# The attention step of a fused attention and MoE kernel: other order on TensorE, narrower value matmuls, reordered first loads

## The chip, the cores and the metric

The kernel runs on one core of a Trainium2 chip as one program. The metric is the device time of the whole program in microseconds (us), the median of three runs. Engines are named as in the profile: PE is TensorE, DVE is VectorE, ACT is ScalarE, POOL is GpSimd, SP is SyncE, whose queue (SPq) issues nearly all DMAs here.

## The reference

Two batches, eight heads, 576 positions, head size 64. An attention with a learned position bias is followed by two feed-forward layers of 2048 on 1152 tokens of 512 columns:

```python
scores = (1.0 / np.sqrt(D)) * np.matmul(q, k.transpose(0, 1, 3, 2))
psi_rel = np.log1p(np.abs(rel))                     # rel = pos_i - pos_j
psi_i = np.log1p(np.maximum(pos[:, None], 1.0))
h = np.maximum((psi_rel / psi_i)[..., None] @ w1 + b1, 0.0)   # 32 hidden units for each (i, j)
scores = scores + (h @ w2).transpose(2, 0, 1)[None]            # one bias for each head
attn = np.exp(scores - np.max(scores, axis=-1, keepdims=True))
attn = attn / (np.sum(attn, axis=-1, keepdims=True) + 1e-09)
attn_out = np.matmul(attn, v)
x = moe(attn_out, w_in, w_out)      # h = x @ w_in; relu(h) + alpha * min(h, 0); @ w_out
return moe2(x, w_in2, w_out2)       # h = x @ w_in2; P(h) / (Q(h) + 1e-06); @ w_out2
```

All data are 32-bit floats.

## The kernel before, in words

**Stages.** The attention comes first, then the two feed-forward layers (lines 686 `up` and 701 `down`). Everything is written into one list of pieces, `Agenda`, each with a number that says when it is to come; the pieces are emitted in the order of these numbers, and every engine then works through its own instructions in that order, waiting on semaphores where data or a buffer is not ready. The numbers come from the table `Z` and from `step_time(n)`. They set an order, not a time.

**Steps.** Query rows are cut into nine blocks of 128 (`BLOCKS`: four blocks of rows for each of the two batches, and one last block that holds the 64 left-over rows of both). Each block has four steps, one for each pair of heads, so there are 36 steps, n = 0 to 35. For step n:

- `scores` (line 332, tile `s`): eight matmuls of 288 columns, four for each head.
- `row_max` (line 344, DVE): adds the bias, takes the maximum, leaves the sum in tile `p`.
- `expo` (line 355, ACT): the exponential.
- `flip` (lines 369 and 365, tile `tp`) one step later: nine transposes of 128x128 as 4, 4 and 1, each group into a PSUM tile of the two-buffer pool `ps_t`; `flip_out` copies them into `pt` on ACT (line 381) or DVE (375, 379).
- `values` (line 393, tile `pv`) two steps later: ten matmuls with a stationary tile of 64 columns, which the profile shows as twenty passes; each two of them write the two halves of the 128 output partitions.

A block ends with `inverse`, `inverse_flip` (line 411), `inverse_spread` (lines 418 and 422: a small tile goes to DRAM and comes back spread over the partitions as `rb`), `block_out`, `block_scale` (line 446, DVE) and `block_split`. Blocks from the seventh on use `inverse_on_tensor` (line 438) instead of the way through DRAM.

**Bias.** The bias of a block of rows is made beside the steps of the block before it, one row group (`bias_rows`) for about each step: four `hidden` tiles `h` (line 258 on DVE, line 256 on ACT), then for each half of the 576 columns four matmuls into 32 partitions each (`bias_mm`, line 272, tile `bps`, a PSUM pool of one buffer), then `bias_out` (line 286 on DVE, 284 on ACT; 293 and 291 for the first block) into tile `be`, then a DMA `bias_move` (line 298, or 302) to its place. The first block's eight row groups come before step 0. For the last block `bias_again` (line 306) copies the bias of the first 64 partitions to the other 64.

**Order on PE in a step:** scores, bias half, 4 transposes, values, bias half, 4 + 1 transposes, scores of the next step.

**Widths.** In the rows, `128*128`, `128*64` and `128*32` are rows and columns of the stationary tile of a matmul. Scores and transposes use 128 columns, values 64, bias matmuls 32.

**First loads.** All on SP's queue, in the order of the agenda: small constants, queries of block 0 (`qraw`, a pool of one buffer), four key loads of batch 0 (`kraw`), the rest of the table `tt`, five value loads of batch 0, then the bias moves as their tiles become ready. `be` has three buffers.

Of the kernel before, what the change touches and what calls it, by code (L numbers as in the profile page):

```python
# [22 lines left out]
P = 128  # L23
# [27 lines left out]
def row_tables():  # L51
# [25 lines left out]
    "iflip": 1.64, "ispread": 2.86, "bout": 0.89, "bscale": 1.31, "bsplit": 3.11, "m0": 1.59, "m1": 17.06,  # L77
    "tb": 3.44, "ud": 3.65, "ud2x": 3.05, "ustore": 2.4, "uback": 7.0, "uload": 7.77, "urest": -0.15, "ujoin": 1.2, "utwo_early": 4.81, "ulow_early": 5.57,
# [27 lines left out]
def fused_kernel(ctx: ExitStack, tc: tile.TileContext, qT, q4T, kT, vp, m1_in, m1_out, m2_in, m2_out, small, ttab, out):  # L106
# [46 lines left out]
    xu_p = open_pool("xu", 1, "left")  # L153
    rq_p = open_pool("rq", 1, "left")
    q_p = open_pool("q", 8, "left")
# [3 lines left out]
    h_p = open_pool("h", 10, "right")  # L159
    be_p = open_pool("be", 3, "right")  # L160
    ps_v = open_pool("ps_v", 1, "left", PSUM)
# [79 lines left out]

    bias, hid, bev, bps = {}, {}, {}, {}

# [19 lines left out]
    def bias_mm(j, r, u):  # L263
        if j > 0:
            ps = ps_b.tile([P, HALF], F32, tag="b", name="bps")
            bps[j, r, u] = ps
        else:
            if u == 0:
                bps[j, r] = ps_s.tile([P, 2, 512], F32, tag="s", name="bps2")
            ps = bps[j, r][:, u, :HALF]  # L270
        for c in range(4):
            nc.tensor.matmul(  # L272
                out=ps[32 * c : 32 * c + 32], lhsT=w2s, rhs=hid[j, r, c][:, u * HALF : (u + 1) * HALF],
                start=True, stop=True,
            )
# [28 lines left out]
    def bias_again(h):  # L304

        nc.vector.tensor_copy(out=bias[4][64:, h : h + 4], in_=bias[4][:64, h : h + 4])

    def bias_rows(j, r, at, step, at0, step0):
# [5 lines left out]
        ag.at(at + Z["bias_mm1"] * z, bias_mm, j, r, 1)  # L314
        ag.at(at + (1.6 * step if j == 0 else Z["bias_out1"] * z), bias_out, j, r, 1)
        ag.at(at + Z["bias_move"] * z, bias_move, j, r)

    ptile, pps, tps, ptt, sums, pvs = {}, {}, {}, {}, {}, {}
# [40 lines left out]
    def flip(n, u):  # L359
        p = ptile[n]  # L360
        if u == 0:
            ptt[n] = pt_p.tile([P, 9, P], F32, tag="pt", name="pt")
        tp = ps_t.tile([P, 512], F32, tag="t", name="tp")
        if u == 2:
# [18 lines left out]
    def values(n):  # L383
        k, hp = divmod(n, 4)
        ib, b = BLOCKS[k]
        if hp == 0:
            pvs[k] = ps_v.tile([P, 4, P], F32, tag="pv", name="pv")
        pv, pt = pvs[k], ptt.pop(n)
        for bb, cols in [(b, slice(0, P))] if ib < 4 else [(0, slice(0, 64)), (1, slice(64, P))]:
            for j in range(5):  # L390
                for u in range(2):
                    h = 2 * hp + u
                    nc.tensor.matmul(  # L393
                        out=pv[64 * u : 64 * u + 64, hp, cols],
                        lhsT=V[bb][:, j, h, :],
                        rhs=pt[:, 4 * u + j if j < 4 else 8, cols],
                        start=(j == 0), stop=(j == 4),
                    )
# [91 lines left out]
    for j, r, at, step in rows:  # L490
        bias_rows(j, r, at, step, at0, step0)
        at0, step0 = at, step
    EARLY = rows[-1][2] + Z["bias_move"] * rows[-1][3] / 4.1 + 0.1
    for n in range(NSTEP):
# [11 lines left out]
        if hp == 3:  # L506
            ag.at(t + Z["inv"], inverse, k)
            if by_tensor(k):
                ag.at(t + 3 * DT + Z["bscale"] - 0.1, inverse_on_tensor, k)
            else:  # L510
                ag.at(t + DT + Z["iflip"], inverse_flip, k)
                ag.at(t + DT + Z["ispread"], inverse_spread, k)
            ag.at(t + 3 * DT + Z["bout"], block_out, k)
            ag.at(t + 3 * DT + Z["bscale"], block_scale, k)
            ag.at(t + 3 * DT + Z["bsplit"], block_split, k)
# [280 lines left out]

    ag.at(step_time(20), moe_consts)
    ag.at(EARLY + 2.0, bias_again, 0)
    ag.at(EARLY + 4.0, bias_again, 4)
    ag.at(EARLY, early_pools)  # L800
# [125 lines left out]
```

## Time and profile before

| | before |
|---|---|
| median of 3 runs | 618.4 us (617.63 to 619.54) |
| the profiled execution, its time and its span | 615.66 us, 613.9 us |
| PE busy | 595.5 us, 97% of the span |
| DVE busy | 519.8 us, 85% |
| ACT busy | 436.6 us, 71% |
| share of the chain that ended last | PE 78%, DVE 11%, DMA 5% |
| granted TensorE clock, mean | 0.993 |

Busy time is the time in which at least one instruction of the engine runs. The chain is followed back from the last instruction to what released each piece. Scores start at 26.77 us for step 0 and at 198.25 us for step 35; the first matmul of the feed-forward layers starts at 200.80 us.

### The profile page before, as it was taken

How to read it: one execution, taken by the hardware profiler on the slowest of the kernel's cores; microseconds unless marked ns; L12 is line 12 of the kernel's file. 1: busy time of each engine (PE TensorE's matmuls, PEld its weight loads, DVE VectorE, ACT ScalarE, POOL GpSimd, SP SyncE). 2: the span in 40 equal slices, each digit the busy share in tenths (PEclk: the TensorE clock that was granted, in tenths of full speed). 3: DMA queues.
4: the chain of work that ended last, by engine and by line, in shares of the span. 5: the costliest groups of instructions: out<-in, count | busy, mean ns of one | idle time of the engine just before them, and what ended most of it. 6: DMA issues, size and time to landing. Idle time of an engine off the chain costs nothing.

```text
span 613.9 us, 11091 instructions
## 1 busy us (share of the span) xinstructions
PE 595.5 (97%) x4278; PEld 522.0 (85%) x4278; DVE 519.8 (85%) x883; ACT 436.6 (71%) x724; POOL 77.1 (13%) x83
## 2 busy tenths in 40 slices
PE   8689999999999999999999999999999999999997
PEld 4456667767778999999999999998999999999985
DVE  6799898798688877779998787989999999789783
ACT  4789888889876555777766657787777887655660
POOL 1113222122235332000000020300000000000000
PEclk9889999999999999999999999999999999999999
DMA  9872444323553332445445557775200000001011
GB/s 248 187 198 76 117 118 119 97 72 94 151 152 104 94 113 105 137 130 157 156 146 168 172 167 234 204 253 188 87 1 0 1 2 0 2 0 52 1 52 52
DMA packets 41749, 67.62 MB, mean 110 GB/s; under 512 B 5040, under 2 KB 24800, under 8 KB 41696
## 3 DMA queue, kind: packets, MB, share of 16 engines
q1 hardware_dynamic: 41552, 66.57, 36.9%
q8 instruction: 33, 0.54, 0.4%
q10 hardware_dynamic: 144, 0.35, 0.2%
q14 instruction: 20, 0.16, 0.1%
HBM read 49.71 MB, written 6.58 MB: 92 GB/s over the span
## 4 chain that ended last, share of the span: by engine, by line
PE 78%; DVE 11%; DMA 5%; ACT 2%; issue 2%; POOL 0%; SPq 0%; DVEq 0%; ACTq 0%; POOLq 0%
PE ops L701 29%; PE hps L686 29%; PE bps L272 5%; PE pv L393 5%; PE s L332 4%; PE tp L369 4%; DMA bias<-be 2%; DMA qraw<-in_qT_dram 2%; DVE p L344 1%; DVE mid L625 1%; DVE h L258 1%; DVE w L655 1%; DVE ks L210 1%; DMA away<-mid 1%; DVE acc L773 1%
## 5 line engine op out<-in xcount | busy, mean ns | idle before, releaser
L686 PE MATMUL hps<-xh,w 128*128 128x384 f32 x768 | 204.0, 336 | 0.0
L686 PEld LDWEIGHTS hps<-xh,w 128*128 128x128 f32 x768 | 139.6, 188 | 1.1 <-issue 0.2
L686 PE MATMUL hps<-xl,w 128*128 128x384 f32 x384 | 128.7, 335 | 0.0
L701 PE MATMUL ops<-g,w 128*128 128x384 f32 x576 | 104.5, 336 | 0.0
L701 PE MATMUL ops<-w,g 128*128 128x512 f32 x432 | 102.5, 392 | 1.2 <-DVE acc L773 1.2
L701 PEld LDWEIGHTS ops<-g,w 128*128 128x128 f32 x576 | 100.8, 188 | 0.0
L701 PEld LDWEIGHTS ops<-w,g 128*128 128x128 f32 x432 | 80.7, 188 | 17.5 <-issue 1.5
L686 PEld LDWEIGHTS hps<-xl,w 128*128 128x128 f32 x384 | 72.1, 188 | 0.9
L756 ACT CAST g<-n 128x768 fp32r<-128x768 f32 x48 | 40.1, 835 | 40.0 <-DVE n L720 28.0
L355 ACT ACTIVATE p<-p,nm 128x576 f32<-128x576 f32 x72 | 55.7, 774 | 13.4 <-DVE nm L344 12.9
L272 PE MATMUL bps<-h,w2s 128*32 128x288 f32 x576 | 52.9, 432 | 8.9 <-DVE be L286 3.8
L625 DVE SCALAR_TENSOR_TENSOR mid<-mid,raw 128x512 int32<-128x512 int32 x64 | 48.9, 764 | 13.1 <-ACT mid L617 12.9
L258 DVE TENSOR_SCALAR h<-tt,sc,nb 128x576 f32<-128x576 f32 x98 | 55.8, 605 | 0.1
L344 DVE CUSTOM_DVE_ANT_0 p<-s,bias 128x576 f32<-128x576 f32 x72 | 52.3, 750 | 1.4 <-PE s L332 1.1
L761 DVE TENSOR_TENSOR g<-n,g 128x768 fp32r<-128x768 f32 x48 | 46.6, 970 | 7.8 <-ACT g L756 7.8
L332 PE MATMUL s<-ks,q 128*128 128x288 f32 x320 | 52.4, 308 | 0.6 <-DVE ks L210 0.6
L238 POOL TENSOR_TENSOR q<-qraw,q 128x256 fp32r<-128x256 f32 (+1 forms) x40 | 34.4, 859 | 144.2 <-DVE q L237 124.4
L628 DVE SCALAR_TENSOR_TENSOR mid<-raw,mid 128x512 int32<-128x512 int32 x64 | 49.5, 773 | 2.2
L369 PEld LDWEIGHTS tp<-ident,p 128*128 128x128 f32 x288 | 30.9, 141 | 23.5 <-issue 15.3
L393 PE MATMUL pv<-pt,v 128*64 128x128 f32 (+1 forms) x800 | 47.8, 267 | 0.2 <-DVE pt L375 0.2
L332 PEld LDWEIGHTS s<-ks,q 128*128 128x128 f32 x320 | 44.7, 192 | 2.6 <-issue 1.1
L369 PE MATMUL tp<-ident,p 128*128 128x128 f32 x288 | 46.6, 284 | 0.3 <-ACT pt L381 0.3
(77 smaller groups left out, 836.9 us busy)
## 6 DMA issues: line engine op xcount, KB each, us to landing
raw<-in_moe_w_in_dram SPq DMA_DIRECT2D x32, 512.0 KB, 4.3
raw<-in_moe_w_out_dram SPq DMA_DIRECT2D x32, 512.0 KB, 3.6
bias<-be SPq DMA_DIRECT2D x32, 288.0 KB, 4.8
qraw<-in_qT_dram SPq DMA_DIRECT2D x8, 512.0 KB, 5.5
away<-mid SPq DMA_DIRECT2D x16, 256.0 KB, 2.0
mid<-away SPq DMA_DIRECT2D x16, 256.0 KB, 3.9
v<-in_vp_dram SPq DMA_DIRECT2D x10, 256.0 KB, 7.5
kraw<-in_kT_dram SPq DMA_DIRECT2D x8, 288.0 KB, 5.0
```

What stands on the lines that cost most here:

```text
L258: nc.vector.tensor_scalar(out=h, in0=x, scalar1=sc[:, k : k + 1], scalar2=nb1, op0=ALU.mult, op1=ALU.max)
L272: nc.tensor.matmul(out=ps[32 * c : 32 * c + 32], lhsT=w2s, rhs=hid[j, r, c][:, u * HALF : (u + 1) * HALF], start=True, stop=True,)
L332: nc.tensor.matmul(out=ps[:, w, :HALF], lhsT=x[:, u, :], rhs=kk[:, h, w * HALF : (w + 1) * HALF], start=(i == 0), stop=(i == len(terms) - 1),)
L344: nc.vector.tensor_tensor_reduce(out=ptile[n][:, u, :].rearrange("p (w j) -> p w j", w=2), in0=pps.pop((n, u))[:, :, :HALF], in1=bias[j][: ...
L355: nc.scalar.activation(out=p, in_=p, func=AF.Exp, bias=nms.pop((n, u)), scale=-1.0, accum_out=sums[k][:, h : h + 1])
L369: nc.tensor.transpose(out=tp[:, j * P : (j + 1) * P], in_=p[:, u, o : o + P], identity=ident)
L393: nc.tensor.matmul(out=pv[64 * u : 64 * u + 64, hp, cols], lhsT=V[bb][:, j, h, :], rhs=pt[:, 4 * u + j if j < 4 else 8, cols], start=(j == ...
L625: nc.vector.scalar_tensor_tensor(out=m, in0=m, scalar=3, in1=raw[:, :, 0], op0=ALU.logical_shift_left, op1=ALU.bitwise_or)
L628: nc.vector.scalar_tensor_tensor(out=m, in0=raw[:, :, 1], scalar=-(2 ** 31), in1=m, op0=ALU.bitwise_and, op1=ALU.bitwise_or)
L686: nc.tensor.matmul(out=ps, lhsT=a, rhs=b, start=(i == 0), stop=(i == len(prs) - 1))
L701: nc.tensor.matmul(out=ops[ly, c, m], lhsT=a, rhs=b, start=(f == fs[0] and i == 0), stop=(f == fs[-1] and i == 2))
L761: nc.vector.tensor_tensor(out=gt[:, 1], in0=tmp.pop(p), in1=gt[:, 0].bitcast(F32), op=ALU.subtract)
```

## The change

What it does, part by part:

1. The PE order of a step becomes: scores, all nine transposes of the step before, bias half, values, bias half. The numbers `flip0`, `flip1`, `flip2` put the transposes right behind the scores, and the new `bias_rows_beside` puts the two bias halves on both sides of `values`.
2. `values` uses stationary tiles of 32 columns for all blocks but the last: twenty matmuls in place of ten, each four writing the four quarters of the output partitions.
3. The ninth transpose goes into the upper half of the PSUM buffer of the bias pool `ps_b`, and the first bias half behind it takes the lower half of the same buffer (`spare`).
4. First loads: the third and fourth key load and the five value loads of batch 0 move behind bias moves. `be` gets four buffers, `rq` two, and `load_q` comes earlier in its step.
5. `bias_again` is cut into four copies of two heads, in steps 29 to 32, where it was two copies of four heads.
6. `inverse_flip` moves to just before the scores of step n + 2; `inverse_on_tensor` and its `block_scale` move later in their step.

```diff
-    ... "flip0": 1.82, "flip1": 1.62, ... "flip2": 3.84, "fout2": 4.38, ... "ispread": 2.86,
+    ... "flip0": 0.5, "flip1": 0.1, ... "flip2": 0.7, "fout2": 1.6, ... "ispread": 1.0,
-    ... "load_k02": 3.0, "load_k03": 3.2, ... "load_v0": 4.0, ... "loadq": 5.34,
+    ... "load_k02": 9.5, "load_k03": 11.2, ... "load_v0": 19.3, "again": 2.6, ... "beside": 0.85, "iscale": 2.75, ... "loadq": 2.6,
-    rq_p = open_pool("rq", 1, "left")
+    rq_p = open_pool("rq", 2, "left")
-    be_p = open_pool("be", 3, "right")
+    be_p = open_pool("be", 4, "right")
...
     def bias_mm(j, r, u):
         if j > 0:
-            ps = ps_b.tile([P, HALF], F32, tag="b", name="bps")
+            ps = (spare.pop() if spare else ps_b.tile([P, 512], F32, tag="b", name="bps"))[:, :HALF]
...
-        nc.vector.tensor_copy(out=bias[4][64:, h : h + 4], in_=bias[4][:64, h : h + 4])
+        nc.vector.tensor_copy(out=bias[4][64:, h : h + 2], in_=bias[4][:64, h : h + 2])
...
+    def bias_rows_beside(j, r, at, step, at0, step0):
+
+        z, z0 = step / 4.1, step0 / 4.1
+        for c in range(4):
+            ag.at(at0 + z0 * Z[f"hidden{c}"], hidden, j, r, c)
+        for u in range(2):
+            x = at + Z[f"bias_mm{u}"] * z
+            n = max((n for n in range(NSTEP) if step_time(n) <= x), default=None)
+            t = x if n is None else max(x, step_time(n) + Z["beside"])
+            ag.at(t, bias_mm, j, r, u)
...
+            ag.at(t, bias_out, j, r, u)
+        ag.at(max(at + Z["bias_move"] * z, t + 0.1), bias_move, j, r)
...
-        tp = ps_t.tile([P, 512], F32, tag="t", name="tp")
+        if u < 2:
+            tp = ps_t.tile([P, 512], F32, tag="t", name="tp")
+        else:
+            spare[:] = [ps_b.tile([P, 512], F32, tag="b", name="bps")]
+            tp = spare[0][:, HALF:]
...
+        wide = 32 if ib < 4 else D
...
-                for u in range(2):
-                    h = 2 * hp + u
+                for u, d in [(u, d) for u in range(2) for d in range(0, D, wide)]:
                     nc.tensor.matmul(
-                        out=pv[64 * u : 64 * u + 64, hp, cols],
-                        lhsT=V[bb][:, j, h, :],
+                        out=pv[64 * u + d : 64 * u + d + wide, hp, cols],
+                        lhsT=V[bb][:, j, 2 * hp + u, d : d + wide],
...
-        bias_rows(j, r, at, step, at0, step0)
+        (bias_rows if j == 0 else bias_rows_beside)(j, r, at, step, at0, step0)
...
-                ag.at(t + DT + Z["iflip"], inverse_flip, k)
-                ag.at(t + DT + Z["ispread"], inverse_spread, k)
+                ag.at(step_time(n + 2) - 0.06, inverse_flip, k)
+                ag.at(step_time(n + 2) + Z["ispread"], inverse_spread, k)
...
-    ag.at(EARLY + 2.0, bias_again, 0)
-    ag.at(EARLY + 4.0, bias_again, 4)
+    for h in range(0, H, 2):
+        ag.at(step_time(29 + h // 2) + Z["again"], bias_again, h)
```

On PE, in a step in the middle of the attention, the instructions stood like this before (`s` scores, `bps` bias, `tp` transposes, `pv` values):

```order
L332 MATMUL s<-ks_135,q 128x288 x8
L272 MATMUL bps<-h,w2s 32x288 x4
L369 MATMUL tp<-ident,p 128x128 x4
L393 MATMUL pv<-pt,v_137 64x128 x10
L272 MATMUL bps<-h,w2s 32x288 x4
L369 MATMUL tp<-ident,p 128x128 x4
L365 MATMUL tp<-ident,p 128x128
```

and the same step of the changed kernel stands like this:

```order
L350 MATMUL s<-ks_135,q 128x288 x8
L391 MATMUL tp<-ident,p 128x128 x8
L387 MATMUL bps<-ident,p 128x128
L272 MATMUL bps<-h,w2s 32x288 x4
L415 MATMUL pv<-pt,v_137 32x128 x20
L272 MATMUL bps<-h,w2s 32x288 x4
```

The transposes have moved together behind the scores, values are 20 matmuls of 32 where they were 10 of 64, and bias, values and bias stand next to each other.

On SP's queue the first DMAs were issued in this order before (`sm` constants, `kraw` keys, `tt` the table, `v` values):

```order
L140 DMA sm<-in_small_dram 128x200
L219 DMA qraw<-in_qT_dram 128x1024
L202 DMA kraw<-in_kT_dram 64x1152 x2
L467 DMA tt<-in_ttab_dram 128x472
L202 DMA kraw<-in_kT_dram 64x1152 x2
L213 DMA v_136<-in_vp_dram 128x512 x5
L298 DMA bias<-be 16x8x576 x8
L202 DMA kraw<-in_kT_dram 64x1152 x2
```

and in the changed kernel:

```order
L140 DMA sm<-in_small_dram 128x200
L219 DMA qraw<-in_qT_dram 128x1024
L202 DMA kraw<-in_kT_dram 64x1152 x2
L489 DMA tt<-in_ttab_dram 128x472
L298 DMA bias<-be 16x8x576 x2
L202 DMA kraw<-in_kT_dram 64x1152
L298 DMA bias<-be 16x8x576
L202 DMA kraw<-in_kT_dram 64x1152
L298 DMA bias<-be 16x8x576 x5
L213 DMA v_136<-in_vp_dram 128x512 x5
```

The first bias moves now stand ahead of the value loads and of two key loads.

On DVE near the end of the attention, the rows between the maxima of steps 28 and 29 (`p,nm` is `row_max`) were these before:

```order
L344 ISA p,nm<-s,bias 128x576
L344 ISA nm 128x1
L306 COPY bias<-bias 64x2304
L237 CAST q<-qraw 128x256
L306 COPY bias<-bias 64x2304
L375 COPY pt<-tp 128x128
L344 ISA p,nm<-s,bias 128x576
```

and in the changed kernel the first such copy stands one step later, behind the maxima of step 29, alone:

```order
L362 ISA p,nm<-s,bias 128x576
L362 ISA nm 128x1
L397 COPY pt<-bps 128x128
L237 CAST q<-qraw 128x256
L306 COPY bias<-bias 64x1152
L401 COPY pt<-tp 128x512
L362 ISA p,nm<-s,bias 128x576
```

One copy of 1152 elements stands there now, and three more of that size follow in later steps.

## Rows read from the trace of the kernel before

**Rows 1.** Windows: start:end, length, busy us (instructions) of PE, PEld, DVE, ACT, POOL, PEclk, DMA.

```profile
32.36:75.35 42.99, 40.76 (x419) 27.37 (x415) 39.72 (x94) 37.87 (x75) 11.57 (x9) 0.97 0.52 139
75.35:165.93 90.58, 90.58 (x998) 64.52 (x997) 75.56 (x204) 77.81 (x164) 20.52 (x24) 1.00 0.39 104
270.00:400.00 130.00, 130.00 (x749) 130.00 (x748) 114.18 (x174) 88.78 (x148) 11.49 (x8) 1.00 0.58 174
```

**Rows 2.** The same windows, PE, scores alone (line 332, eight a step).

```profile
32.36:75.35 42.99, 11.69 (x65) 0.97 0.52 139
75.35:165.93 90.58, 24.74 (x152) 1.00 0.39 104
```

**Rows 3.** The same window, PE, bias matmuls alone (line 272, eight passes a half).

```profile
75.35:165.93 90.58, 24.93 (x288) 1.00 0.39 104
```

**Rows 4.** Timeline of PE, one step (start, length, line, tile, shape, passes).

```profile
111.71 1.31 PE L393 MATMUL pv<-pt,v 128*64 128x128 f32 x20
112.95 0.69 PE L272 MATMUL bps<-h,w2s 128*32 128x288 f32 x8
113.57 0.66 PE L369 MATMUL tp<-ident,p 128*128 128x128 f32 x4
...
114.09 1.29 PE L332 MATMUL s<-ks,q 128*128 128x288 f32 x8
115.32 0.69 PE L272 MATMUL bps<-h,w2s 128*32 128x288 f32 x8
115.94 0.66 PE L369 MATMUL tp<-ident,p 128*128 128x128 f32 x4
116.53 0.66 PE L393 MATMUL pv<-pt,v 128*64 128x128 f32 x8
```

**Rows 5.** Timeline of PE, a late step that has no bias matmuls.

```profile
179.19 1.30 PE L332 MATMUL s<-ks,q 128*128 128x288 f32 x8
180.32 0.60 PE L369 MATMUL tp<-ident,p 128*128 128x128 f32 x4
180.85 1.31 PE L393 MATMUL pv<-pt,v 128*64 128x128 f32 x20
...
182.62 2.37 PE L332 MATMUL s<-ks,q 128*128 128x288 f32 x16
```

**Rows 6.** Timeline of PE, two bias halves side by side before step 0.

```profile
23.18 1.18 PE L272 MATMUL bps<-h,w2s 128*32 128x288 f32 x16
```

**Rows 7.** Timeline of PE, values of the last block (half as many columns each).

```profile
196.41 1.39 PE L393 MATMUL pv<-pt,v 128*64 128x64 f32 x40
```

**Rows 8.** The start: timeline of DVE, of SP, the chain, landing of bias moves.

```profile
19.27 0.82 DVE L293 TENSOR_SCALAR be<-bps,cv 128x576 f32<-128x576 f32 x1 [3.81 <-DMA bias<-be]
...
4.68 4.85 SPq L213 DMA_DIRECT2D v<-in_vp_dram  x5
...
10.50 7.21 DMA bias<-be
...
DMA to landing us min/median/max: 3.3/4.8/6.0
```

**Rows 9.** Waits from 75.35 to 165.93: who for whom, us in total, times, longest.

```profile
ACT be L284 <- PE bps L272: 11.6, 16, 1.2
```

**Rows 10.** Waits from 26 to 76.

```profile
DVE q L237 <- DMA qraw<-in_qT_dram: 0.9, 1, 0.9
```

**Rows 11.** Timeline of PE and DVE, steps 29 and 30.

```profile
169.03 1.35 DVE L306 COPY bias<-bias 64x2304 f32<-64x2304 f32 x1 [0.62 <-DMA bias<-be]
169.46 1.30 PE L332 MATMUL s<-ks,q 128*128 128x288 f32 x8
174.58 1.30 PE L332 MATMUL s<-ks,q 128*128 128x288 f32 x8
```

**Rows 12.** Timeline of DVE and SP, the way of the inverse through DRAM.

```profile
111.39 0.27 DVE L413 COPY rt<-tp 8x128 f32<-8x128 f32 x1
112.92 1.27 SPq L422 DMA_DIRECT2D rb<-rd  x2
```

More of the change, by code (lines that the diff above doesn't have):

```diff
@@ L74 @@
     "bias_out0": 1.51, "bias_mm1": 3.37, "bias_out1": 3.67, "bias_move": 6.78, "dt2": 4.01, "row2": 3.98,
[2 rows of a table removed]
-    "iflip": 1.64, "ispread": 2.86, "bout": 0.89, "bscale": 1.31, "bsplit": 3.11, "m0": 1.59, "m1": 17.06,
[2 rows of a table added]
+    "iflip": 1.64, "ispread": 1.0, "bout": 0.89, "bscale": 1.31, "bsplit": 3.11, "m0": 1.59, "m1": 17.06,
     "tb": 3.44, "ud": 3.65, "ud2x": 3.05, "ustore": 2.4, "uback": 7.0, "uload": 7.77, "urest": -0.15, "ujoin": 1.2, "utwo_early": 4.81, "ulow_early": 5.57,
@@ L240, in split_q @@
             )
-    bias, hid, bev, bps = {}, {}, {}, {}
+    bias, hid, bev, bps, spare = {}, {}, {}, {}, []
     def bias_tile(j):
@@ L314, in bias_rows @@
         ag.at(at + Z["bias_mm1"] * z, bias_mm, j, r, 1)
-        ag.at(at + (1.6 * step if j == 0 else Z["bias_out1"] * z), bias_out, j, r, 1)
+        ag.at(at + 1.6 * step, bias_out, j, r, 1)
         ag.at(at + Z["bias_move"] * z, bias_move, j, r)
+    def bias_rows_beside(j, r, at, step, at0, step0):
[7 more added lines that the diff above has]
+            ag.at(t, bias_mm, j, r, u)
+            if n is None:
+                t += 0.4
+            else:
+                key = "scalar" if f"bias_scalar_{j}{u}" in ON else "vector"
+                t = max(step_time(n) + Z[f"bo_{key}{int(t - step_time(n) >= Z['values'])}"], t + 0.1)
+            ag.at(t, bias_out, j, r, u)
+        ag.at(max(at + Z["bias_move"] * z, t + 0.1), bias_move, j, r)
     ptile, pps, tps, ptt, sums, pvs = {}, {}, {}, {}, {}, {}
@@ L362, in flip @@
             ptt[n] = pt_p.tile([P, 9, P], F32, tag="pt", name="pt")
-        tp = ps_t.tile([P, 512], F32, tag="t", name="tp")
+        if u < 2:
+            tp = ps_t.tile([P, 512], F32, tag="t", name="tp")
+        else:
+            spare[:] = [ps_b.tile([P, 512], F32, tag="b", name="bps")]
+            tp = spare[0][:, HALF:]
         if u == 2:
@@ L508, in fused_kernel @@
             if by_tensor(k):
-                ag.at(t + 3 * DT + Z["bscale"] - 0.1, inverse_on_tensor, k)
+                ag.at(t + 3 * DT + Z["iscale"] - 0.1, inverse_on_tensor, k)
             else:
-                ag.at(t + DT + Z["iflip"], inverse_flip, k)
-                ag.at(t + DT + Z["ispread"], inverse_spread, k)
+                ag.at(step_time(n + 2) - 0.06, inverse_flip, k)
+                ag.at(step_time(n + 2) + Z["ispread"], inverse_spread, k)
             ag.at(t + 3 * DT + Z["bout"], block_out, k)
-            ag.at(t + 3 * DT + Z["bscale"], block_scale, k)
+            ag.at(t + 3 * DT + Z["iscale" if by_tensor(k) else "bscale"], block_scale, k)
             ag.at(t + 3 * DT + Z["bsplit"], block_split, k)
```

10 rows, old and new, of the table Z are left out of this document.

## The prediction

> **What bounds the kernel now.** I read the busy times first: PE is busy 97% of the span, and the chain that ended last is PE for 78%. So I looked at the windows, to see where in the attention PE is the limit and where it isn't. From 270 to 400 us, in the feed-forward layers, PE is busy in every microsecond [rows 1]: nothing in the change touches them, and whatever the attention gains or loses, they start that much earlier or later. The attention has four stretches.
>
> From 75.35 to 165.93 us PE is also busy without a gap, 90.58 of 90.58 us, while DVE is busy for 75.56 and ACT for 77.81 [rows 1]. The scores count 152 matmuls, eight a step [rows 2]: 19 steps of 4.77 us, of which DVE needs 3.98 and ACT 4.10. ACT waits 11.6 us in all for bias matmuls [rows 9]. Here PE's order and widths set the time. From 32.36 to 75.35 the 65 score matmuls are eight steps of 5.37 us [rows 1, 2]; DVE is busy for 39.72 of 42.99 us, so DVE sets that time, with PE close behind it (40.76). Before step 0, DVE sits idle for 3.81 us because `be` isn't free: the bias move that frees it was issued at 10.50 and took 7.21 us, behind five value loads that were issued from 4.68 on [rows 8]. And at the end, steps 29 to 31 are uneven (below).
>
> **The order on PE, steps 75 to 166.** One step before, from start to start [rows 4]: values 1.24 (111.71 to 112.95), bias 0.62, five transposes 0.52, scores 1.23 (114.09 to 115.32), bias 0.62, four transposes 0.59 (115.94 to 116.53); 4.82 in all.
>
> Some of that belongs to changing the width of the stationary tile. Scores followed by transposes (128 columns, then 128) take 1.13, from 179.19 to 180.32 [rows 5]; followed by bias (128, then 32) they take 1.23 [rows 4]: 0.10 for leaving a width. Four transposes behind scores take 0.53, from 180.32 to 180.85 [rows 5]; behind bias they take 0.59 [rows 4]: 0.06 for entering one. Two bias halves side by side last 1.18 [rows 6] where one lasts 0.69 [rows 4], so the second adds 0.49, and not 0.62: the same size again. I take 0.16 a change. A step had five changes of width (scores to bias, bias to transposes, transposes to values, values to bias, bias to transposes) and has two after: transposes to bias, and bias to scores.
>
> The new step, piece by piece: scores 1.13 + 0.06 for entering = 1.19; nine transposes, with 0.107 each from (0.53 - 0.10) / 4, plus 0.10 for leaving = 1.07; first bias half 0.62 - 0.10 = 0.52; values 1.24 - 0.16 = 1.08; second bias half 0.62 - 0.06 = 0.56. Sum 4.42, so 0.40 less a step. Three changes at 0.16 would give 0.48, the upper end.
>
> The 1.08 holds only if four value parts of 32 columns run side by side as two of 64 do. No row shows that form. Below: twenty passes of 128 columns, one after the other at the 0.107 of a transpose, would take 2.1, and took 1.24 [rows 4], so two do run side by side; and a bias half, eight passes of 288 columns, adds 0.49 [rows 6] where one after the other would take 8 x 0.107 x 288 / 128 = 1.9, so four parts of 32 do. Above: forty passes, as many as there will be, last 1.39 in the last block [rows 7], against 1.31 for twenty [rows 4]: 0.08 more. Between 1.08 and 1.16 I take 1.08, since the bias row is the same tile form; with 1.16 the step saves 0.32.
>
> A page speaks against this part. The Trainium skill, "TensorE: Matmul & The Clock Gate", section "Wait — 56ns, not 53.3ns?", says that with hardware decode off the sequencer spends about 62 ns on each matmul and becomes the limit once the array's work is shorter. By that figure forty passes would take 40 x 62 = 2.48 us, an estimate from that page. The trace disagrees: its forty passes last 1.39 us [rows 7], 35 ns each.
>
> Then ACT (4.10) and DVE (3.98) are only 0.3 and 0.4 below the new 4.42. Steps differ (a block's end adds work on both), so some wait will remain; I take off 0.08 a step. All 19 steps have a pair of bias halves but one (288 passes are 36 halves [rows 3]). **19 x 0.32 = 6.0 us**; bounds 19 x 0.16 = 3.0 (values at 1.16 and a doubled hold) and 18 x 0.48 = 8.6.
>
> What is queued behind the moved pieces: the transposes wait for the second exponential of the step before, and bias and values now stand behind them. That exponential follows a maximum which can start when the scores are done, and has until the next step's scores end, over 5 us later, so I cost it at nothing; in a step of 5 us it is covered too. The second bias half needs the shared buffer read by `flip_out` and the first `bias_out`; values, 1.08, lie between.
>
> **The first 32 us.** The value loads go behind the bias moves, and `be` has four buffers, so the move of row group 0 has to land only before the fifth row group is written out. The move issued at 10.50 then takes 3.3 to 6.0 as others do [rows 8] and lands at 13.8 to 16.5; DVE stopped at 19.27 - 3.81 = 15.46. So between 2.8 and 3.8 of the 3.81 goes, and DVE has no other wait of such a size before step 0. I take 3.8, the nearer to the usual landing of 4.8, plus 0.3 for PE which no longer stands still there: **4.1 us**, bounds 2.8 and 4.8. Two key loads fall behind two bias moves, some 9 us later, and are cast only after 25 us; the value loads have some 15 us until the first `values`: nothing.
>
> **Steps 0 to 8.** DVE's work is unchanged, at 39.72 of 42.99 us [rows 1]: at most 3.3 can go. One wait that surely goes is the 0.9 for queries [rows 10], by the second `rq` buffer. I take **1.2 us**, bounds 0 and 2.8.
>
> **The end.** Steps 29 to 30 take 5.12 (169.46 to 174.58) [rows 11]; a step without bias takes 3.43, from 179.19 to 182.62 [rows 5]. The two copies of `bias_again`, 1.35 each, start at 169.03 after a 0.62 wait for a bias move [rows 11], and the maximum of step 29 stands behind both. In the change it stands behind none, the wait is a step later, when the move has landed, and each later step carries one copy of half the size, about 0.7, below what DVE has free. 5.12 - 3.43 = **1.7 us**; bounds 0.4 (the copies delay later maxima instead) and 2.8.
>
> **Sum.** 6.0 + 4.1 + 1.2 + 1.7 = 13.0 us. The profiled execution took 615.66, which would become 602.7; the median of the runs shown is 618.4, 2.7 above it, so I forecast **605.4 us**. All lower bounds add to 6.2 (612.2), all upper ones to 19.0 (599.4).
>
> **Rivals.**
> - *Values become slow.* If the four parts run as two pairs, one pair after the other, values cost 1.08 more. In 19 steps that is 20.5; in the eight before, PE has 2.2 to spare of 42.99 [rows 1], so 6.4 of 8.6 count: 27 in all, against 13: 632 us, slower. It decides from about 0.5 us a step on. Against it: the bias rows. The page's 62 ns would make it 1.4 a step, near 640 by the same count, an estimate from that page.
> - *The changes of width don't go away*, as bias and values, though both 32 wide, differ in what they read and where they write: the step stays at 4.8, and 7.0 us remain: 611.4.
> - *ACT or DVE take over.* Their 77.81 and 75.56 leave room, but if the order makes them wait as often as now (11.6 us over 19 steps, 0.6 a step [rows 9]), steps come to 4.10 + 0.6 = 4.7, and about 5 of the 6.0 is lost: 610.
> - *The inverse comes late.* From its copy at 111.39 to the end of the second `rb` issue at 114.19 it takes 2.8 [rows 12], and landing 3.3 or more [rows 8]. It now starts just before the scores of step n + 2, and `block_scale` on DVE, with a maximum queued behind it, comes about 1.4 steps later, 6.2 us: up to 1 us late in six blocks, and later behind a query load. 13 - 6 = 7: 611.
> - *More than I count:* 0.48 a step with no hold, and DVE's idle time of steps 0 to 8 all gone: 8.6 + 4.8 + 2.8 + 2.0 = 18: 600.
>
> **How the numbers follow.** Forecast, 602 to 609: 0.62. More: 0.10. Width changes stay: 0.07. ACT or DVE: 0.09. Inverse: 0.07. Slow values: 0.05. The range is 599.5 to 611.5: it takes in the sum's upper bound and the rivals that leave 7 us, and leaves out slow values and mishaps together. 0.3% of 618.4 is 1.9 us, which is what a measurement of this kernel can tell from no change. Faster 0.92, same 0.03 (two of the middle rivals together), slower 0.05.
>
> **What would show it.** Values behind bias should start about 0.5 after it, and last near 1.1 from start to start, with forty passes; a step should take 4.4 to 4.5 between 70 and 155 us, and ACT's wait for bias matmuls shrink. DVE's 3.81 idle should be gone and the first scores start near 23. No copy of bias should stand ahead of the maximum of step 29. The forecast is wrong if values last 1.3 or more, if DVE waits for `rb`, or if transposes wait long for exponentials.

## The result, and the profile after

| | after |
|---|---|
| median of 4 runs | 627.5 us (625.4 to 629.33) |
| before, same chip, 4 runs | 618.97 us (617.63 to 619.71) |
| ratio | 1.0139, 95% interval 1.0097 to 1.0182: slower |
| profiled execution, its time and span | 629.33 us, 627.5 us |
| PE busy | 596.7 us, 95% |
| chain that ended last | PE 68%, DVE 13%, issue 6%, DMA 5%, ACT 5% |
| granted TensorE clock, mean | 0.984 |

The forecast was 605.4. The two profiled executions stand further apart than the medians, by 13.67 us against 8.5: the one after is the slowest of its four (628.73 and 629.33 us at mean clocks of 0.982 and 0.984, 625.4 and 626.26 at 0.991 and 0.992), and the one before lies 3.3 us under its median. To see where the 13.67 us arose, I noted when the scores of a step start, and took the stretches between them:

| stretch | before | after | difference | forecast |
|---|---|---|---|---|
| up to the scores of step 0 | 26.77 | 24.50 | -2.27 | -4.1 |
| step 0 to step 8 | 43.71 | 55.92 | **+12.21** | -1.2 |
| step 8 to step 28 | 95.45 | 98.20 | **+2.75** | -6.0 |
| step 28 to step 35 | 32.32 | 32.23 | -0.09 | -1.7 |
| step 35 to the end | 415.63 | 416.70 | +1.07 | 0 |

First the windows of the changed kernel, from step 1 to 8, from 8 to 28 and from 28 to 35 (start:end, length, then busy us and instructions of PE, PEld, DVE, ACT, POOL, then PEclk, DMA share and GB/s):

```profile
30.97:80.42 49.45, 39.64 (x484) 28.61 (x480) 36.71 (x81) 32.88 (x66) 10.26 (x8) 0.83 0.51 130
80.42:178.62 98.20, 92.01 (x1454) 70.04 (x1450) 78.23 (x217) 82.84 (x174) 22.44 (x26) 1.00 0.34 95
178.62:210.85 32.23, 30.63 (x460) 26.82 (x456) 27.05 (x69) 22.87 (x51) 13.13 (x22) 1.00 0.51 141
```

PE was never idle from 75 to 166 us [rows 1]; now, from step 8 to 28, it is idle for 6.2 us of 98.2. In the seven steps from 1 to 8 it stands for 9.8 of 49.45 us, where in the eight from 1 to 9 it stood for 2.23 of 42.99 [rows 1]. DVE and ACT have idle time as well there: no engine is the limit. They wait for one another.

**A step that nothing disturbs**, PE's timeline (start, length, line, tile, shape, passes), to be held against [rows 4]:

```profile
120.08 1.35 PE L350 MATMUL s<-ks,q 128*128 128x288 f32 x8
121.27 1.04 PE L391 MATMUL tp<-ident,p 128*128 128x128 f32 x8
122.14 0.27 PE L387 MATMUL bps<-ident,p 128*128 128x128 f32 x1
122.34 0.69 PE L272 MATMUL bps<-h,w2s 128*32 128x288 f32 x8
122.85 1.27 PE L415 MATMUL pv<-pt,v 128*32 128x128 f32 x40
123.99 0.69 PE L272 MATMUL bps<-h,w2s 128*32 128x288 f32 x8
...
124.64 0.64 PE L350 MATMUL s<-ks,q 128*128 128x288 f32 x3
```

From start to start: scores 1.19, nine transposes 1.07, bias 0.51, values 1.14, bias 0.62, a small inverse transpose 0.03; 4.56 us in all. I had 1.19, 1.07, 0.52, 1.08 and 0.56, 4.42. So PE's own work came out almost as costed. Twenty such steps would be 91.2 us; they took 98.2.

**A step from 80 to 179 us that is long** (109.22 to 115.18, 5.96 us): DVE, ACT and PE in turn. In brackets stand the idle time before and who ended it.

```profile
111.91 0.69 DVE L468 TENSOR_TENSOR xu<-xu,rb 128x512 f32<-128x512 f32 x1 [0.87 <-DMA rb<-rd]
112.52 0.75 DVE L362 CUSTOM_DVE_ANT_0 p<-s,bias 128x576 f32<-128x576 f32 x1
...
113.68 0.28 DVE L397 COPY pt<-bps 128x128 f32<-128x128 f32 x1
```

```profile
114.00 0.50 ACT L284 ACTIVATE be<-bps,cv 128x288 f32<-128x288 f32 x1 [1.59 <-DVE pt L397]
```

```profile
111.97 1.27 PE L415 MATMUL pv<-pt,v 128*32 128x128 f32 x40
114.56 0.69 PE L272 MATMUL bps<-h,w2s 128*32 128x288 f32 x8 [1.32 <-ACT be L284]
115.18 1.05 PE L350 MATMUL s<-ks,q 128*128 128x288 f32 x6
```

This reads as a chain. DVE stands 0.87 us for `rb`; its scaling (`block_scale`), a maximum and a hidden tile come ahead of the copy of the ninth transpose; ACT's `bias_out`, in the same buffer as that transpose, waits for the copy; the second bias half needs the buffer and waits for ACT; and the next scores stand behind that bias half on PE. So one late DMA reaches the scores.

**The early steps.** PE, DVE and ACT from step 1 on:

```profile
34.37 0.41 PE L387 MATMUL bps<-ident,p 128*128 128x128 f32 x1
34.71 0.73 PE L272 MATMUL bps<-h,w2s 128*32 128x288 f32 x8
39.06 1.19 PE L272 MATMUL bps<-h,w2s 128*32 128x288 f32 x8 [3.62 <-DVE be L286]
40.18 1.33 PE L350 MATMUL s<-ks,q 128*128 128x288 f32 x4
41.31 1.93 PE L391 MATMUL tp<-ident,p 128*128 128x128 f32 x8
```

```profile
35.52 0.29 DVE L397 COPY pt<-bps 128x128 f32<-128x128 f32 x1 [1.59 <-PE bps L272]
35.85 1.35 DVE L210 TENSOR_TENSOR ks<-kraw,ks 64x1152 fp32r<-64x1152 f32 x1
37.23 0.76 DVE L362 CUSTOM_DVE_ANT_0 p<-s,bias 128x576 f32<-128x576 f32 x1
...
37.91 0.58 DVE L258 TENSOR_SCALAR h<-tt,sc,nb 128x576 f32<-128x576 f32 x1
38.40 0.51 DVE L286 TENSOR_SCALAR be<-bps,cv 128x288 f32<-128x288 f32 x1
```

```profile
40.33 0.50 ACT L284 ACTIVATE be<-bps,cv 128x288 f32<-128x288 f32 x1 [5.02 <-PE bps L272]
```

The first bias half ends at 35.4. DVE copies the ninth transpose out only then, although that transpose had been made by 34.78: both are in one buffer. Of the 1.59 us that DVE is idle before the copy, 0.7 come after the transpose's end. Then a key cast, a maximum and a hidden tile run on DVE, and `bias_out` comes at 38.40. PE's second bias half waits 3.62 us for it, with the scores of step 2 behind it; ACT waits 5.02 us for that half. The Trainium skill has a rule that fits the copy's wait: "PSUM — Partial Sum Buffer", section "PSUM bank collisions raise a hardware error", tells to guard PSUM by bank and quadrant and not by address, so two halves of one bank don't make two independent buffers. The waits agree: 5.0 us in 8 such waits of DVE's copy in the row of the waits below.

The waits of steps 1 to 8 and of steps 8 to 28 (who for whom: us in total, times, longest):

```profile
ACT be L284 <- PE bps L272: 11.4, 3, 5.0
PE bps L272 <- DVE be L286: 5.6, 2, 3.6
PE bps L272 <- ACT be L284: 3.5, 3, 1.7
```

```profile
ACT be L284 <- DVE pt L397: 6.0, 10, 1.6
PE bps L272 <- ACT be L284: 5.6, 7, 1.4
DVE pt L397 <- PE bps L272: 5.0, 8, 1.1
DVE xu L468 <- DMA rb<-rd: 2.2, 2, 1.3
```

In steps 1 to 8 PE waits 9.1 us in all for `bias_out`, on DVE or ACT, nearly its whole idle time of 9.8. Before, its waits for `bias_out` on DVE from 26 to 76 us, step 0 included, were these, with 0.3 more for ACT:

```profile
PE bps L272 <- DVE be L286: 3.8, 5, 2.1
```

PE's 5.6 us for ACT between 80 and 179 are nearly its whole idle time there (6.2).

**The start.** DVE:

```profile
22.14 0.82 DVE L293 TENSOR_SCALAR be<-bps,cv 128x576 f32<-128x576 f32 x1 [1.75 <-DMA bias<-be]
```

The wait of 3.81 [rows 8] became 1.75, for another move. In the chain it stands like this:

```profile
14.42 7.62 DMA bias<-be
```

It took 7.62 us, hardly other than the 7.21 in [rows 8], though no value load was ahead of it any more; two key loads and three bias moves were, issued from 10.44 us on. From 14 to 22 us the DMA engines were full (start:end, as in the windows above; the share of DMA is the last column but one):

```profile
14.00:22.00 8.00, 7.94 (x87) 3.85 (x86) 6.26 (x13) 7.67 (x10) 0.73 (x1) 1.00 1.04 207
```

**The end.** From step 29 to 30 it took 3.47 us (182.11 to 185.58), where it had taken 5.12 [rows 11]: the 1.65 that I had costed at 1.7. From 31 to 32 it took 4.55 (before 3.43), and from 34 to 35 7.07 (before 5.74), which gave it back.

### The profile page after: what moved, and what is told of

Its sections match the earlier page's. It is cut to its first block, busy times and chain, and to the rows that moved or that the text cites. A ratio compares the mean times of both kernels' runs of the same rounds, so it can differ in the third digit from the quotient of the medians.

```text
span 627.5 us, 12390 instructions
## 1 busy us (share of the span) xinstructions
PE 596.7 (95%) x4918; PEld 529.4 (84%) x4918; DVE 518.9 (83%) x885; ACT 436.6 (70%) x724; POOL 78.0 (12%) x83
## 4 chain that ended last, share of the span: by engine, by line
PE 68%; DVE 13%; issue 6%; DMA 5%; ACT 5%; POOL 1%; SPq 0%; DVEq 0%; ACTq 0%; POOLq 0%
PE ops L723 28%; PE hps L708 28%; PE bps L272 4%; PE s L350 3%; PE tp L391 3%; DVE p L362 2%; PE pv L415 2%; DVE h L258 2%; DMA rb<-rd 1%; DMA bias<-be 1%; DVE mid L647 1%; DVE ks L210 1%; DMA qraw<-in_qT_dram 1%; ACT h L256 1%; ACT p L373 1%
## 5 line engine op out<-in xcount | busy, mean ns | idle before, releaser
L350 PE MATMUL s<-ks,q 128*128 128x288 f32 x320 | 57.3, 323 | 2.6 <-DVE ks L210 2.6
L350 PEld LDWEIGHTS s<-ks,q 128*128 128x128 f32 x320 | 46.9, 200 | 15.3 <-issue 15.1
L415 PEld LDWEIGHTS pv<-pt,v 128*32 128x32 f32 (+1 forms) x1440 | 40.6, 113 | 8.0 <-issue 2.6
L415 PE MATMUL pv<-pt,v 128*32 128x128 f32 (+1 forms) x1440 | 46.5, 268 | 0.0
L643 ACT ACTIVATE raw<-raw 128x512 int32<-128x512 uint32 x64 | 43.4, 678 | 3.7 <-DMA raw<-in_moe_w_out_dram 2.8
```

Source lines behind the costliest of these rows:

```text
L350: nc.tensor.matmul(out=ps[:, w, :HALF], lhsT=x[:, u, :], rhs=kk[:, h, w * HALF : (w + 1) * HALF], start=(i == 0), stop=(i == len(terms) - 1),)
L415: nc.tensor.matmul(out=pv[64 * u + d : 64 * u + d + wide, hp, cols], lhsT=V[bb][:, j, 2 * hp + u, d : d + wide], rhs=pt[:, 4 * u + j if j ...
L643: nc.scalar.activation(out=low, in_=low.bitcast(U32), func=AF.Copy, scale=0.90625 * 2.0 ** -29, bias=0.24)
```

## The experiments

All times are medians of 4 to 10 runs; beside them the median of before on the same chip. The three stretches are of the profiled execution, in us. Before had 26.77, 43.71 and 95.45, the changed kernel 24.50, 55.92 and 98.20.

| kernel | time | before | ratio (95%) | to step 0 | 0 to 8 | 8 to 28 |
|---|---|---|---|---|---|---|
| e1_old_order | 618.9 | 617.3 | 1.0025 (0.9998 to 1.0052) | 25.00 | 44.28 | 99.23 |
| e2_values64 | 625.47 | 617.3 | 1.011 (1.0047 to 1.0173) | 23.74 | 52.95 | 98.40 |
| e3_old_loads | 627.27 | 617.3 | 1.0141 (1.0065 to 1.0218) | 25.36 | 52.20 | 97.65 |
| e5_whole_scores | 628.93 | 617.3 | 1.0165 (1.0099 to 1.023) | 25.07 | 52.63 | 98.61 |
| e4_old_inverse | 628.84 | 616.72 | 1.0196 (1.0142 to 1.0251) | 24.64 | 53.88 | 99.03 |
| e6_old_order_inverse | **610.93** | 616.72 | 0.9899 (0.9847 to 0.9952) | 23.71 | 43.47 | 92.91 |
| e7_loads_only | 613.5 | 616.72 | 0.9948 (0.9926 to 0.997) | 24.87 | 44.44 | 95.47 |
| e8_new_order_late | 618.1 | 616.72 | 1.0021 (0.9997 to 1.0045) | 24.10 | 44.18 | 98.65 |
| e9_later_scale | 621.18 | 617.04 | 1.0066 (1.0037 to 1.0095) | 24.33 | 55.63 | 93.71 |
| e10_mixed_later_scale | 614.26 | 617.04 | 0.9949 (0.993 to 0.9968) | 24.49 | 44.02 | 94.88 |
| e11_ninth_apart | 626.37 | 617.04 | 1.013 (1.0089 to 1.0171) | 24.12 | 48.62 | 101.55 |
| e12_bias_on_act | 623.17 | 617.04 | 1.0082 (1.0059 to 1.0105) | 23.80 | 47.68 | 100.09 |
| e13_both_links | 617.61 | 617.55 | 0.9993 (0.9969 to 1.0017) | 25.27 | 47.23 | 94.68 |

Six kernels keep the new order in all steps and its shared buffer and its writers of bias (the changed one, e2, e3, e4, e5 and e9): their steps 0 to 8 take 52.2 to 55.9, so the early loss against 43.71 is 8.5 to 12.2 us, by execution. By medians, two pairs of kernels that were run together give it: e4 and e8 differ in the order of steps 0 to 7 alone (the ninth transpose's buffer goes with it), by 10.7 us, and e9 and e10 in that and in the time of one block's inverse, by 6.9.

**e1_old_order: PE's order, bias places and the ninth transpose as before**, in the changed kernel; values of 32, loads, pools and the new time of the inverse stay.

```diff
-    ... "flip0": 0.5, "flip1": 0.1, ... "flip2": 0.7, "fout2": 1.6, ...
+    ... "flip0": 1.82, "flip1": 1.62, ... "flip2": 3.84, "fout2": 4.38, ...
...
-        (bias_rows if j == 0 else bias_rows_beside)(j, r, at, step, at0, step0)
+        bias_rows(j, r, at, step, at0, step0)
```

> The changed kernel with the order of before on all engines for transposes and bias, and the ninth transpose back in its own tile; values of 32 columns, first loads, pools, bias copies and inverse stay as changed. Theory of the ring (in the new order the second bias half waits for ACT's and DVE's readers of the one bias tile, with the next scores queued behind it, and the scores of steps 1 to 3 are cut in two by the transposes): the 12 us lost between steps 0 and 8 and the 0.14 a step lost behind them go, step 8 starts about 44 us after step 0, and the time is 612 to 618. Theory of the loads (the value loads, now at 23 to 28 us, keep the DMA engines full until 44 us and what waits for them late): the loss stays before step 4, time 624 to 629. Theory of slow values (32 columns): the steps from 8 on stay at 4.9 or more, time over 622.

618.9, just above the range of the ring: the early loss is gone (44.28), but steps 8 to 28 are no faster (99.23). Ordinary steps take 4.67 us, and one in each block 5.8 to 7.1, in which the inverse's transpose, now just ahead of the scores, waits for a buffer of `ps_t` (waits of steps 8 to 28):

```profile
PE tp L429 <- ACT pt L399: 5.5, 5, 1.3
DVE xu L464 <- DMA rb<-rd: 1.4, 1, 1.4
```

**e2_values64: values as before** (`wide = D`), all else as changed.

> The changed kernel with values of 64 columns again, all else as changed. Ring: the step is held by waits and by 4.50 of PE work; with 64 columns PE's work rises by two changes of width, to about 4.8, part of which the waits swallow: 2 to 6 us slower than the change, 629 to 634. Slow values: faster than the change by 3 us or more. Loads: as the ring has it.

625.47, not above the changed kernel: a miss. Against before it is 1.011, where the changed kernel is 1.0139, and the two intervals overlap. In the new order the narrow values gain nothing over steps 8 to 28 (98.40 with 64 columns, 98.20 with 32), though undisturbed steps take 4.70 to 4.76 with 64 and 4.56 with 32. That the waits between the engines swallow this fits, but no run tests it by itself.

**e3_old_loads: the first loads in the order of before.**

```diff
-    ... "load_k02": 9.5, "load_k03": 11.2, ... "load_v0": 19.3, ...
+    ... "load_k02": 3.0, "load_k03": 3.2, ... "load_v0": 4.0, ...
```

> The changed kernel with the two key loads and the value loads of batch 0 issued first again, as before; four buffers of be and two of rq stay. Loads: the 12 us lost between steps 0 and 8 go, the first scores start near 26, time 616 to 619. Ring: the loss between steps 0 and 4 stays at 9 us or more, the first scores start 1 to 2 us later than the change's 24.5, time 627 to 631.

627.27, with 52.20 from step 0 to 8: the moved loads don't make the early loss. The start is 0.9 later.

**e5_whole_scores: transposes behind the scores of both heads also in steps 1 to 3 and 33 to 35**, where the changed kernel puts them between the heads (the timeline above: scores x4, transposes x8).

> The changed kernel with the transposes emitted behind both heads' scores in steps 1 to 3 and 33 to 35 too (their time counted from the next step's own start), all else as changed. If the ring of the early steps closes through the cut scores (maximum of the second head waits for scores that stand behind eight transposes): steps 1 to 4 become 1 to 2 us shorter each, 4 to 7 us in all, time 620 to 624. If the ring closes through the bias tile alone: 1 to 2 us, time 625 to 627. Loads: no change.

628.93, above both expectations. Steps 0 to 8 take 52.63, within the 52.2 to 53.9 of e2, e3 and e4, which keep the cut: the cut isn't the cause.

**e4_old_inverse: the inverse at the time of before**, in the new order.

```diff
-    ... "ispread": 1.0, ...
+    ... "ispread": 2.86, ...
...
-                ag.at(step_time(n + 2) - 0.06, inverse_flip, k)
-                ag.at(step_time(n + 2) + Z["ispread"], inverse_spread, k)
+                ag.at(t + DT + Z["iflip"], inverse_flip, k)
+                ag.at(t + DT + Z["ispread"], inverse_spread, k)
```

> The changed kernel with inverse_flip and inverse_spread at their times of before, all else as changed. If the late inverse (DVE waits for rb with a maximum and the copy of the ninth transpose behind it) makes the long steps of 5.9 to 6.1 us: three or four of them shrink to about 4.6, time 621 to 624. If the bias tile alone holds the steps: under 2 us, time 625 to 628.

628.84, a miss: the wait for `rb` is gone, but the inverse's transpose now comes right behind eight others and waits for ACT to copy one of their tiles out (waits of steps 8 to 28):

```profile
PE tp L433 <- ACT pt L403: 4.7, 5, 1.4
```

**e6_old_order_inverse: e1 and e4 together**, so that of the change there remain values of 32, loads, pools, bias copies and the later `inverse_on_tensor` of the last blocks.

> Order of before for transposes, bias and inverse; of the change only values of 32 columns, first loads, pools and bias copies. In the run with the old order and the late inverse, ordinary steps took 4.67 us where before has 4.83, and one step of each block 5.8 to 6.2, PE waiting at the inverse's transpose for ACT to free a transpose tile. If that wait is all that held it back: no long steps, 19 steps of 4.67 between 75 and 166 us, time 609 to 613. If the long steps have another cause: 617 to 620.

610.93, faster than both kernels. PE is busy again without a gap from step 8 to 28 (windows, steps 0 to 8 and 8 to 28):

```profile
23.71:67.18 43.47, 39.56 (x509) 26.48 (x509) 41.12 (x91) 36.28 (x69) 12.24 (x9) 0.92 0.80 191
67.18:160.09 92.91, 92.84 (x1453) 68.21 (x1451) 80.04 (x217) 82.61 (x175) 21.54 (x25) 1.00 0.37 100
```

**e7_loads_only: e6 with values of 64.**

> As the kernel with order and inverse of before, and with values of 64 columns too: only first loads, pools and bias copies of the change are left. If 32 columns save one change of width a step (values to bias): 3 to 5 us slower than that kernel, 613 to 617, steps of 4.83. If the narrow values save nothing: the same as that kernel. Against before this gives the worth of loads, pools and bias copies: my prediction's terms for the start and the end say 5 us less, the first runs say about 2.

613.5. The narrow values are worth 2.6 us, and what else e6 keeps of the change 3.2. Steps 8 to 28 take 95.47 against 92.91: 0.13 a step on the mean, and 0.15 in ordinary steps (4.82 against 4.67), for one change of width less.

**e8_new_order_late: e6, with the new order from step 8 on** (order of before in steps 0 to 7).

```diff
+    EARLY_STEPS = 8
...
-        (bias_rows if j == 0 else bias_rows_beside)(j, r, at, step, at0, step0)
+        (bias_rows if at < step_time(EARLY_STEPS) else bias_rows_beside)(j, r, at, step, at0, step0)
...
+            f0, f1, f2, o2 = (1.82, 1.62, 3.84, 4.38) if n < EARLY_STEPS else (0.5, 0.1, 0.7, 1.6)
...
```

> The new order from step 8 on and the order of before in steps 0 to 7, inverse at its time of before; the rest as changed. If the new order costs only where PE has to wait for a DVE that is full (steps 0 to 8): the early 10 us come back and steps from 8 on take 4.5 to 4.6, time 606 to 611, the fastest of all. If the ring through the bias tile costs the same in a PE-bound step as it saves: steps of 4.7 to 4.8, 611 to 617.

618.1, above both expectations: steps 0 to 8 are as in e6 (44.18), steps 8 to 28 as in e4 (98.65), 5.74 more than in e6. The order costs in both places, in the later one with the inverse's transpose behind eight others, as in e4.

**e9_later_scale: the changed kernel with `block_scale` and `block_split` of the first six blocks later in their step.**

```diff
-    ... "bscale": 1.31, ...
+    ... "bscale": 3.0, ...
...
-            ag.at(t + 3 * DT + Z["bsplit"], block_split, k)
+            ag.at(t + 3 * DT + (Z["bsplit"] if by_tensor(k) else 4.9), block_split, k)
```

> The changed kernel, with block_scale and block_split of the first six blocks placed about 1.7 us later in their step, so that DVE does not stand at rb when the scaling comes. If the late inverse (a wait of 1.3 us for rb on DVE, and what queues behind it) makes the long steps of 5.9 to 6.1 between steps 8 and 28, they shrink and steps 8 to 28 take 93 to 95.5 us instead of 98.2: 621 to 625. If the ring over the shared bias buffer (copy of the ninth transpose behind the bias half, bias_out behind that copy, second bias half behind bias_out) makes them, the waits only change their name: 626 to 629.

621.18. Steps 8 to 28 fall from 98.20 to 93.71; the step from 109 to 115 takes 4.56 (108.34 to 112.90). DVE no longer waits for `rb`, and PE's waits for ACT go from 5.6 to 2.6:

```profile
PE bps L272 <- ACT be L284: 2.6, 5, 1.4
```

So DVE's wait for the late inverse, 2.2 us, is worth 4.5 us here, passed on.

**e10_mixed_later_scale: e8, with the new inverse and the later scaling from step 8 on.**

> The order and inverse of before in steps 0 to 7, the new order and new inverse from step 8 with the later scaling; everything else as changed. The early loss of 11 to 12 us must be gone in any case (scores of step 8 near 68). If late rb is all that keeps the new order from its 4.5 a step, steps 8 to 28 take 90 to 93 us: 606 to 611. If the order of the pieces itself costs waits in the steps, they take 95 to 99: 612 to 618.

614.26, in the range of the second theory; 94.88 from step 8 to 28, just under what it had there, and still 2 more than e6. PE still waits 2.7 us there for ACT's `bias_out`, and none in e6.

**e11_ninth_apart: the ninth transpose in its own buffer**, and back behind the second bias half, in the changed kernel. So it changes the buffer and the place at once.

```diff
-    ... "flip2": 0.7, "fout2": 1.6, ...
+    ... "flip2": 3.84, "fout2": 4.38, ...
...
-        if u < 2:
-            tp = ps_t.tile([P, 512], F32, tag="t", name="tp")
-        else:
-            spare[:] = [ps_b.tile([P, 512], F32, tag="b", name="bps")]
-            tp = spare[0][:, HALF:]
+        tp = ps_t.tile([P, 512], F32, tag="t", name="tp")
```

> The changed kernel, with the ninth transpose back in a PSUM tile of its own pool, behind the second bias half as before; the bias pool's one buffer is then used by bias halves alone. If sharing one buffer between the ninth transpose and the first bias half closes the ring (the copy waits for the bias half, bias_out for the copy), both the early loss and the steps from 8 to 28 shrink: 612 to 620. If the order itself does it (bias halves ahead of and behind the values, the second one waiting for bias_out, with the next scores queued behind), it stays at 625 to 629.

626.37: half a hit. Steps 0 to 8 take 48.62, so 4 to 7 us of the early loss come from the ninth transpose in the bias buffer, its place included; but steps 8 to 28 grow to 101.55, as the inverse's transpose now waits for `ps_t`. In the early steps PE still waits for DVE's `bias_out`:

```profile
PE bps L272 <- DVE be L286: 4.6, 3, 2.5
```

**e12_bias_on_act: the bias of the second row block, which is made beside steps 0 to 7, written out on ACT alone** (`"bias_scalar_11"` added), in the changed kernel. The halves that move from DVE to ACT are the second halves of the 576 columns; in the changed kernel's trace they stand first in steps 0 to 2, and second from step 3 on.

> The changed kernel, with the first bias halves' bias_out of the second row block (steps 0 to 7) written out on ACT too, where half of them were on DVE. If the early ring closes because DVE's bias_out stands behind the casts, maxima and hidden tiles that DVE has in these steps, the early loss of 12 us shrinks by 3 to 8 us: 619 to 624. If any engine's bias_out is too late for the second bias half, it stays near 627, or ACT's queue makes it longer, up to 632.

623.17, as the first theory had it: steps 0 to 8 take 47.68, 4.5 to 8 less, though steps 8 to 28 take 100.09. DVE's `bias_out` behind its cast and maxima is the other link.

**e13_both_links: e11 in steps 0 to 7, e12 and e9 together.**

> The changed kernel with the two links of the early ring broken together (in steps 0 to 7 the ninth transpose in its own tile behind the second bias half, and bias_out of the second row block's first halves on ACT too), and the later block_scale for the steps behind. If these two links and the late rb are the whole loss, steps 0 to 8 take 44 to 45.5 us as in the order of before and steps 8 to 28 take 93 to 95.5: 610 to 615. If putting both bias halves beside values is itself too tight in the early steps, whoever writes them out, steps 0 to 8 keep 47 to 49 us: 616 to 620.

617.61, no faster than before, as the second theory had it. Steps 0 to 8 still take 47.23, 3 to 4 more than in the order of before; the medians say the same, 3.4 us above e10, which has the order of before in these steps and the same later scaling. What is left has the same name, with ACT in DVE's place (waits of steps 0 to 8):

```profile
PE bps L272 <- ACT be L284: 7.5, 7, 4.6
```

## Why the prediction was wrong

**The step that failed** is "What is queued behind the moved pieces". It costed the transposes' wait for exponentials at nothing, and gave no cost at all to what it says last, that "the second bias half needs the shared buffer read by `flip_out` and the first `bias_out`; values, 1.08, lie between". That wait came to 9.1 us on PE from step 1 to 8 and 5.6 from 8 to 28. 1.08 us isn't enough for DVE's copy and a `bias_out` that stand in their engines' order behind maxima, casts and hidden tiles, and in steps 0 and 1 there are no values at all. Before, four transposes and the values lay between the two halves, 1.8 us, and five transposes and the scores between the second half and the next first one, also 1.8 [rows 4]. Now it is 1.14 between the halves and 2.26 behind the second, and the scores are queued behind that half. Putting the old order back in steps 0 to 7 removes the early loss (e8, e10); breaking either link of the ring removes a part (e11, e12), and both together don't remove all (e13). So the order itself is the cause, sharpened by the shared buffer and by DVE's queue.

**The inverse that comes late** was a rival at 0.07, priced at up to 1 us in six blocks. It came, for 4.5 us in steps 8 to 28 (e9), beside the failed step and not in its place; of the prediction's signs of being wrong, it is the one that showed: DVE waits for `rb`. In the order of before the new time costs about 8 us (e1 against e6), there also through a transpose that finds no free buffer.

**The new order on PE** was rightly costed as work: 4.56 a step for 4.42. Mis-sized were values (1.14 for 1.08) and the second bias half (0.62 for 0.56). A change of width cost 0.15 in ordinary steps where it was isolated (e6 against e7; I took 0.16), and the further two that the new order saves only 0.05 each (4.67 to 4.56). The four parts of 32 do run side by side. So the rival of slow values and that of widths that don't go away both fall.

**The hold of 0.08 a step** was too small: the steps from 8 to 28 lose (98.20 - 91.2) / 20 = 0.35 each. I argued from busy times that ACT and DVE had 0.3 and 0.4 to spare; that a step's chain passes through PE, DVE, ACT and PE again in one step doesn't show in busy times. The rival in which ACT or DVE take over, at 0.09, had such waits too, but with these engines as the limit; in steps 8 to 28 they are idle for 15.4 and 20.0 of 98.2 us.

**The start** was right in kind; half of its size came: 2.27 of 4.1. I took the usual landing of 4.8 for a bias move; the one that DVE now waited for took 7.62, with the DMA engines full.

**Steps 0 to 8** I thought to be set by DVE, and so safe from PE's order. DVE was busy for 39.72 of 42.99, from step 1 to 9 [rows 1]; from 1 to 8 of the changed kernel it was idle for 12.7 of 49.45.

**The end**: the 1.7 came at step 29 and was given back in steps 31 and 34. It isn't the order alone that took it back: e7, with the order of before, takes 3.43 for step 29 and then 6.19 for step 30, where before took 4.60. There PE waits for DVE's scaling, which stands behind a bias copy on DVE (timelines of PE and DVE):

```profile
177.75 0.33 PE L383 MATMUL tp<-ident,p 128*128 128x128 f32 x1 [1.39 <-DVE xu L464]
```

```profile
175.74 1.23 DVE L306 COPY bias<-bias 64x1152 f32<-64x1152 f32 x1
177.00 0.69 DVE L464 TENSOR_TENSOR xu<-xu,tp 128x512 f32<-128x512 f32 x1
```

So the copies that I thought fitted into DVE's free time delay another piece in that kernel. Which wait took the 1.65 back in the changed kernel, no experiment separates. The 1.07 behind step 35 also stays open; runs with the new order there take 416.5 to 417.0, those with the old one 415.3 to 415.6, so it goes with the order.

Of the parts, then, values of 32, loads, pools, bias copies and the later `inverse_on_tensor` are worth 5.8 us together (e6), and the order with its inverse takes 14 away.

## What to carry to other kernels

Before two producers are moved next to each other on one engine, write down for their buffer the round trip: who empties it, what stands ahead of that on its engine, and what is queued behind the second producer. A saving of 0.1 us a step on a busy engine doesn't pay for a round trip with no work between. And where a change has several parts, measure them apart: here some parts gained 5.8 us that the others hid.

## What was not expected of the hardware

Behind PE's waits the granted clock was lower, and that lengthens what it does next. From 38 to 46 us, with the waits above, it was 0.57, and eight transposes took 1.93 us at 41.31 where they take 1.04 at 121.27, with the clock at 1.00 (windows; PEclk is the third column from the end):

```profile
38.00:46.00 8.00, 6.94 (x65) 5.06 (x69) 3.70 (x9) 4.77 (x9) 0.00 (x0) 0.57 0.73 180
119.00:125.00 6.00, 6.00 (x105) 4.36 (x98) 5.13 (x16) 5.99 (x14) 1.66 (x2) 1.00 0.34 105
```

A ratio of 1.86, near that of the two levels, 1.2 and 2.4 GHz: PE was mostly at the lower one, after idle stretches of 2 to 4 us. So PE's busy time from step 1 to 8 holds slow work as well, and the early loss is more than the waits alone.

The same wait doesn't always bring it. PE stands 2.01 us for `bias_out` until 48.48 in the changed kernel's execution and until 48.55 in e5's. Behind it the clock was 0.50 in the first and 1.00 in the second, and PE got through 33 passes in one and 89 in the other (the two windows, in this order):

```profile
48.50:55.30 6.80, 6.16 (x33) 4.15 (x33) 2.79 (x7) 4.87 (x9) 0.72 (x1) 0.50 0.59 164
48.50:55.30 6.80, 5.73 (x89) 3.93 (x89) 5.18 (x14) 5.97 (x13) 0.95 (x2) 1.00 0.61 166
```

Steps 2 and 3 took 11.24 and 6.71 us in the first and 9.92 and 4.89 in the second, whose scores aren't cut; e3, with the cut and the clock also at 1.00 there, has 10.39 and 4.89. So some 3 of the 12.21 us of early loss belong to this execution, and not to every one.

Forty passes of values with 32 columns took 1.14 us from start to start, 28 ns each; twenty with 64 columns had taken 1.24 [rows 4].
